# Unit solves moved to VectorE, x placed by products, weight sums on GpSimd, and spare products in TensorE's first waits

## The chip, the core and the metric

The kernel runs on one core of a Trainium2 chip. The metric is the time of one execution on the device in microseconds (us); the median of repeated runs is given. The core has five engines that run side by side and wait for each other through semaphores: TensorE (PE in the profile; its weight loads are PEld), VectorE (DVE), ScalarE (ACT), GpSimd (POOL) and SyncE (SP), which here only issues DMAs. Each engine works through its own queue in order.

## The reference

Two blocks follow each other. The first is a recurrence over 768 tokens for 4 batches x 8 heads with a state of 40 x 40:

```python
for t in range(S):
    y[:, :, t] = np.einsum('bhd,bhde->bhe', rt, state)
    Sa = np.einsum('bhde,bhe->bhd', state, at)
    state_decay = state * wt[:, :, None, :] - np.einsum('bhd,bhe->bhde', Sa, bt)
    state = state_decay + np.einsum('bhd,bhe->bhde', vt, kt)
```

Its output, 3072 tokens x 320 columns, is the x of the second block, a mixture of four experts with 1024 hidden columns, all in float32:

```python
p = domain_probs / (domain_probs.sum(-1, keepdims=True) + 1e-09)
for e in range(E):
    out += p[:, e:e + 1] * (np.maximum(x @ w1[e], 0.0) @ w2[e])
```

## The kernel before, in words

**Units.** The sequence is cut into 12 chunks of 64 tokens. A unit is one chunk of two batches, so there are 24 units (`NU`); unit u has chunk u // 2, and a chunk's two units hold its four batches. Units 0 and 1 start from an empty state (`q.start`).

**Stages of a unit.** `within` (L338) reads the inputs: it transposes W (pw), scans it along time on VectorE to products of decays (G, L346), transposes them back (pg), scales A, K and B with them (L359 to L392, with a reciprocal at L364), transposes the results (pAT, pNT, pKT) and makes the products inside the chunk: F and E (pfe), pev, and the causal scores pc. `substitute` (L437) solves a triangular system of 32 x 32 blocks: it copies the diagonal blocks out of F (L441), transposes them (M, L445), takes two rows at a time (L458, L461) and then steps through the rows, each step a product (L470) and a sum. On VectorE the sum is one reduction (L480), on GpSimd two additions (L483). Its argument `eng` says which of the two does it. `merge` (L490) joins the two blocks to the whole inverse: two VectorE transposes give Qc and QTc (L495, L497), GpSimd copies QTc to QT (L503), and TensorE products pY (L510) and pQ (L522) with ScalarE copies between give the rest of QT. `step` (L528) carries the state over the chunk: prn, psat (with pst, the part for the state), pxr, pdy, then on VectorE Y (L607 to L612) and the new state (L617, L618). At last it brings Y into `xT`, the layout in which the mixture reads x. In unit 0 this is done by twelve matrix instructions with a 0/1 matrix `pick` (pxT, L624) and a ScalarE copy (L628); in all others by twelve DMAs from SyncE (L636).

**The mixture.** Units 0 and 1 have a mixture of their own (`mixture_of_unit`): per expert `ups` makes the hidden layer in two pieces (ph, L651 and L659, then a Relu on ScalarE, L664), `down` multiplies it with w2 (po, L698), and VectorE adds the result to the output (L675, L677). From chunk 1 on both units of a chunk go together (`mixture_of_chunk`), and the down product is done in seven products of halves instead of eight (L763). For that, `add_weights` (L726) makes five sums and differences of the w2 halves of each expert once, 128 x 640 elements each, on VectorE (L735). They overwrite halves of w2 and buffers that held w1 pieces, `pick` and the probabilities, so each set comes after the last reader of those.

**Order.** The stages are generators. A list written out by hand at the end of the kernel runs them piece by piece: units 0 to 2 one by one, then a loop over u in which the work of units u to u+3 is interleaved. Between them `gap(n)` puts pieces of the mixture from the list `todo`: one piece where 4u+n is in `sparse`, else two; `weights_at` says in which gap which expert's weight sums are made. A scheduler may still move instructions, except those given to `keep_in_program_order`. TensorE's queue is strictly in the order that results. SyncE's queue holds the loads of a unit's six inputs, the w1 pieces, w2, the x placements and the stores in one line. Banks of PSUM for all small products come from one pool of five (`big`).

**Which engine solves.** Unit 0's solve is on VectorE, those of units 1 and 2 on GpSimd, those of units 3 to 5 on VectorE, the rest on GpSimd.

Of the kernel before, what the change touches and what calls it, by code (L numbers as in the profile page):

```python
# [15 lines left out]
def kernel(  # L16
# [320 lines left out]
    def within(q):  # L337
# [16 lines left out]
        nc.vector.tensor_tensor(out=q.gl[:], in0=q.gl[:], in1=G[:, :, L - 1:L], op=ALU.mult)  # L354
        yield

        pg = by(turn("pg", tok(G))[:], 64)[:, :, 0:D]
        gp = sb.tile([P, H, D], FP32, name="gp")
        ins = nc.vector.tensor_tensor(out=gp[:], in0=pg, in1=n["W"][:, :, 0:D], op=ALU.mult)  # L359
        if q.u == 1:  # L360
# [76 lines left out]
    def substitute(q, eng):  # L437

        blocks = sb.tile([P, H, Q], FP32, name="blocks")
        for i in range(P // Q):  # L440
            ins = eng.tensor_copy(out=blocks[quarter(i)], in_=q.F[quarter(i), :, quarter(i % 2)])  # L441
            tc.keep_in_program_order(ins)
        M = sb.tile([P, Q, Q], FP32, name="M")
        cols = blocks[:].rearrange("p h c -> p c h")[:, :, None, :].to_broadcast([P, Q, 4, H])
        ins = nc.vector.transpose(out=M[:], in_=cols)  # L445
        if q.u == 1 or eng is nc.vector:
            tc.keep_in_program_order(ins)


        pairs = M[:].rearrange("p (c two) r -> p c two r", two=2)  # L450
        on_diag = M[:].rearrange("p c r -> p (c r)")[:, Q + 1::2 * (Q + 1)]
        nc.vector.memset(on_diag, 0.0)

        Z = sb.tile([P, 4, Q // 4, Q], FP32, name="Z")
        q.Z = Z[:, 0]
        by_second = Z[:, 1:3].rearrange("p x k r -> p (x k) r")
        below = M[:].rearrange("p c r -> p (c r)")[:, 1::2 * (Q + 1)]
        nc.vector.tensor_tensor(  # L458
            out=by_second, in0=pairs[:, :, 1, :], in1=below[:, :, None].to_broadcast([P, Q // 2, Q]), op=ALU.mult,
        )  # L460
        nc.vector.tensor_tensor(out=pairs[:, :, 0, :], in0=pairs[:, :, 0, :], in1=by_second, op=ALU.add)  # L461
        at_once = eng is nc.vector
        for x in (0, 3) if at_once else (0,):
            tc.keep_in_program_order(eng.tensor_copy(out=Z[:, x], in_=unit_cols[:]))
        for j in range(0, Q, 2):
            if j == Q // 2:
                yield
            n, m = j // 4 + 1, Q - 1 - j
            here = 3 * (j // 2 % 2) if at_once else 0
            ins = eng.tensor_tensor(  # L470
                out=Z[:, 1:3, 0:n, j + 1:Q], in0=M[:, j:j + 2, None, j + 1:Q].to_broadcast([P, 2, n, m]),
                in1=Z[:, here, 0:n, j:j + 2].rearrange("p k x -> p x k")[:, :, :, None].to_broadcast([P, 2, n, m]),
                op=ALU.mult,
            )
            if j in (0, Q // 2):
                tc.keep_in_program_order(ins)
            z = Z[:, :, 0:n, j + 1:Q]
            if at_once:
                terms = z[:, 0:3] if here == 0 else z[:, 1:4]
                eng.tensor_reduce(out=z[:, 3 - here], in_=terms.rearrange("p x k r -> p k r x"), op=ALU.add, axis=AX.X)  # L480
            else:
                for x in range(1, 3):
                    eng.tensor_tensor(out=z[:, 0], in0=z[:, 0], in1=z[:, x], op=ALU.add)  # L483
        if at_once:

            odd, even = (Z[:, x].rearrange("p k (r four) -> p k r four", four=4)[:, :, :, 1:3] for x in (3, 0))
            eng.tensor_copy(out=even, in_=odd)
        yield
# [41 lines left out]
    def step(q, xT):  # L530

        st = [state[bb] for bb in q.b]
        if q.start:
            RH = q.EV
        else:
            p = banks("prn")
            prh = quadrants(p, 0, BY_TOKENS, D, lambda j, s, i: (
                s, i ^ s, j, of_pairs(q.AT, s, j, i), st[i][half(s), j, 0:D],
            ))

            psn = quadrants(p, NJ * D, BY_PAIRS, 64, lambda j, s, i: (
                s, d_half(j, s), 2 * i + j % 2, st[i][half(s), j, :], ident[half(s), half(s)],
            ))
            RH = RHs()
            for s in range(2):
                nc.vector.tensor_tensor(
                    out=of_slot(RH[:], s)[:, :, 0:D], in0=prh[s], in1=of_slot(q.EV[:], s)[:, :, 0:D], op=ALU.add,
                )
            SN = sb.tile([P, 2, 2 * 2, 64], FP32, name="SN", tag="step", bufs=3)
            for s in range(2):  # L550
                nc.scalar.copy(out=SN[:, s], in_=psn[s])
# [6 lines left out]
        ))  # L558
        SX = SXs()
        if not q.end:  # L560
            pst = quadrants(p, NJ * L, BY_TOKENS, D, lambda j, s, i: (
                i ^ s, i, j, q.QT[half(i ^ s), head(j, s), :], RH[half(i ^ s), head(j, s), 0:D],
            ))
        SaT = sb.tile([P, NJ, 2, L], FP32, name="SaT", tag="step", bufs=3)
# [53 lines left out]
                nc.vector.tensor_tensor(out=x, in0=x, in1=gl[:, :, i, :].to_broadcast([P, NJ, D]), op=ALU.mult)  # L618
        yield

        if q.u == 0:
            px = big("pxT")
            for n, (g, j) in enumerate(PLACES):
                nc.tensor.matmul(  # L624
                    out=px[:, g * P:(g + 1) * P], lhsT=pick[:, n, :], rhs=Y[:, j].rearrange("p i t -> p (i t)"),
                    start=(n == 0 or PLACES[n - 1][0] != g), stop=(n + 1 == len(PLACES) or PLACES[n + 1][0] != g),
                )
            nc.scalar.copy(out=xT, in_=px[:, 0:3 * P].rearrange("p (g t) -> p g t", g=3))  # L628
        for h in range(H if q.u else 0):
            lo = h * D  # L630
            while lo < (h + 1) * D:
                g, o = divmod(lo, P)
# [92 lines left out]
    def add_weights(e):  # L725

        b = {(q, x): of_w2(e, q, x) for q in range(2) for x in range(2)}
        for to, x, y, op in (
            (of_sums(e, 0), b[0, 0], b[1, 1], ALU.add),
            (of_sums(e, 1), b[0, 0], b[0, 1], ALU.add),  # L730
            (of_sums(e, 2), b[1, 0], b[1, 1], ALU.add),
            (b[0, 1], b[0, 1], b[1, 1], ALU.subtract),
            (b[1, 0], b[1, 0], b[0, 0], ALU.subtract),
        ):
            tc.keep_in_program_order(nc.vector.tensor_tensor(out=to, in0=x, in1=y, op=op))  # L735

    def mixture_of_chunk(qs, xT):

# [83 lines left out]
    def begin_step(u):  # L822
# [3 lines left out]
        q.xT = chunks_x[q.c][:, :, q.bp * P:(q.bp + 1) * P]  # L826
        return step(q, q.xT)

    ws = [within(units[u]) for u in range(3)]
    run(ws[0], 2)  # L830
    load(units[1], "ABKVR")
    run(ws[1], 1)
    run(ws[0], 2)
    run(substitute(units[0], nc.vector))
    run(ws[0], 1)
# [5 lines left out]
    for e in range(2):  # L841
        load_piece()
        load_piece()
        load_w2(e)
    run(ws[1], 1)
    load(units[2], "ABK")
    load_piece()
    for e in range(2, E):
# [3 lines left out]
    run(ws[1], 1)  # L852
    run(s)
    run(ws[1], 1)
    run(substitute(units[1], nc.gpsimd))
    mixture_of_unit(units[0])
    normalize()
    run(ws[2], 1)
    run(ws[1])
    mix(1)  # L860
    run(ws[2], 2)
    mix(1)
    run(ws[2], 2)
    mix(1)
    m, s = merge(units[1]), begin_step(1)
    run(m, 1)
    run(ws[2], 1)
    load(begin(3), srcs)
    run(substitute(units[2], nc.gpsimd))
    run(m)  # L870
    mix(1)
    run(s, 2)
    mix(1)
    w_next, solve = ws[2], iter(())

    sparse = [4 * u + n for u in range(1, 4) for n in range(4)] + [16]

    weights_at = {4 * 2 + 2: 0, 4 * 3 + 0: 1, 4 * 3 + 2: 2, 4 * 3 + 3: 3}
    for u in range(1, NU):
        q = units[u]  # L880
        m = s_next = w = iter(())
# [74 lines left out]
```

## Time and profile before

| what | value |
|---|---|
| median of 3 runs | 1180.26 us (1180.16 to 1181.2) |
| span of the profiled run | 1179.7 us |
| TensorE busy | 1129.8 us, 96% |
| weight loads | 1005.5 us, 85% |
| VectorE busy | 698.1 us, 59% |
| ScalarE busy | 364.5 us, 31% |
| GpSimd busy | 462.4 us, 39% |
| DMA | 108.03 MB, mean 92 GB/s |

The page also cuts the span into 40 slices of 29.5 us. A digit is a busy share in tenths; PEclk is the clock granted to TensorE.

```profile
PE   4789996999999999999999999999999999999998
DVE  6633787856646655755656566566466557543333
POOL 4165000044734734625536436447347356250000
PEclk8689997999999999999999999999999999999999
DMA  4782633333333333342342332333333331221330
```

The first eight slices differ from the rest: TensorE has gaps there, its clock is below full in several slices, and the DMAs are fullest in the third. A matrix product of float32 with a 128 x 128 weight shows up as two instructions in the profile, so twelve in the profile are six in the kernel.

### The profile page before, as it was taken

What the parts mean: (1) busy time and instruction counts of PE and PEld (TensorE: products, weight loads), DVE (VectorE), ACT (ScalarE), POOL (GpSimd) and SP (SyncE); (2) the same over time, 40 slices, a digit from 0 to 9 for tenths busy, and PEclk for the clock granted to TensorE, in tenths of its full rate; (3) what the DMA queues carried; (4) which work ended last, traced back from release to release, by engine and by line L of the source; (5) the groups of instructions that cost most, each with busy time, mean ns of one, the idle gap of its engine ahead of it and who ended that gap; (6) DMA issues with size and microseconds to landing.
All of it is one profiled execution on the core that took longest, in us unless ns stands there. A gap on an engine that the chain in (4) does not pass through costs nothing.

```text
span 1179.7 us, 38554 instructions
## 1 busy us (share of the span) xinstructions
PE 1129.8 (96%) x16272; PEld 1005.5 (85%) x16272; DVE 698.1 (59%) x1503; ACT 364.5 (31%) x910; POOL 462.4 (39%) x1200
## 2 busy tenths in 40 slices
PE   4789996999999999999999999999999999999998
PEld 3668785899989989898998989999888998988887
DVE  6633787856646655755656566566466557543333
ACT  2323342333332333333333333333323333221110
POOL 4165000044734734625536436447347356250000
PEclk8689997999999999999999999999999999999999
DMA  4782633333333333342342332333333331221330
GB/s 67 200 239 68 141 64 86 78 108 68 95 94 84 96 95 81 92 103 73 95 95 63 108 89 73 107 78 89 90 93 90 93 91 58 76 86 51 103 89 12
DMA packets 220246, 108.03 MB, mean 92 GB/s; under 512 B 164090, under 2 KB 193450, under 8 KB 220074
## 3 DMA queue, kind: packets, MB, share of 16 engines
q1 hardware_dynamic: 220074, 105.56, 34.9%
q8 instruction: 129, 2.11, 0.7%
q14 instruction: 43, 0.35, 0.1%
HBM read 97.04 MB, written 3.93 MB: 86 GB/s over the span
## 4 chain that ended last, share of the span: by engine, by line
PE 86%; DVE 5%; POOL 3%; SPq 2%; issue 2%; DMA 1%; ACT 1%; POOLq 0%; DVEq 0%; ACTq 0%
PE p L763 27%; PE ph L659 27%; PE ph L651 8%; PE pdy L326 3%; PE po L698 2%; PE pfe L326 2%; PE prn L326 2%; POOL Z L483 2%; PE psat L326 2%; PE pxr L326 2%; SPq L188 1%; PE pQ L522 1%; PE pY L510 1%; POOL Z L470 1%; PE pc L326 1%
## 5 line engine op out<-in xcount | busy, mean ns | idle before, releaser
L659 PE MATMUL ph<-xT,w1p 128*128 128x256 f32 (+1 forms) x1520 | 342.8, 378 | 0.2 <-issue 0.2
L659 PEld LDWEIGHTS ph<-xT,w1p 128*128 128x128 f32 x1520 | 274.1, 190 | 62.8 <-issue 25.5
L757 DVE TENSOR_TENSOR a<-hs 128x512 f32<-128x512 f32 x220 | 149.9, 698 | 196.4 <-ACT hs L664 196.3
L483 POOL TENSOR_TENSOR Z<-Z 128x54 f32<-128x54 f32 (+14 forms) x640 | 217.4, 340 | 50.2
L664 ACT ACTIVATE hs<-ph 128x512 f32<-128x512 f32 (+1 forms) x208 | 117.4, 564 | 324.6 <-PE ph L659 323.5
L470 POOL TENSOR_TENSOR Z<-M,Z 128x62 f32<-128x62 f32 (+7 forms) x320 | 154.2, 482 | 89.5 <-DVE M L461 66.0
L677 DVE SCALAR_TENSOR_TENSOR osb<-p,gate,osb 128x320 f32<-128x320 f32 (+1 forms) x242 | 108.4, 486 | 110.4 <-PE p L763 103.2
L763 PE MATMUL p<-sums,a 128*128 128x160 f32 x1056 | 164.8, 299 | 0.0
L763 PEld LDWEIGHTS p<-sums,a 128*128 128x128 f32 x1056 | 152.9, 190 | 2.2
L441 POOL COPY blocks<-F 32x256 f32<-32x256 f32 x80 | 32.3, 404 | 276.6 <-ACT F L416 274.1
L651 PE MATMUL ph<-xT,w1p 64*128 64x256 f32 (+1 forms) x760 | 109.2, 399 | 4.9 <-issue 4.9
L503 POOL COPY QT<-QTc 32x256 f32<-32x256 f32 x96 | 37.7, 393 | 170.6 <-DVE QTc L497 160.7
L763 PE MATMUL p<-w,hs 128*128 128x160 f32 x704 | 102.8, 299 | 0.0
L763 PE MATMUL p<-w,a 128*128 128x160 f32 x704 | 102.8, 299 | 0.0
L763 PEld LDWEIGHTS p<-w,hs 128*128 128x128 f32 x704 | 100.3, 190 | 2.2
L763 PEld LDWEIGHTS p<-w,a 128*128 128x128 f32 x704 | 98.0, 190 | 0.0
L651 PEld LDWEIGHTS ph<-xT,w1p 64*128 64x128 f32 x760 | 67.3, 188 | 17.7 <-issue 7.8
L445 DVE STREAM_TRANSPOSE M<-blocks 128x1024 f32<-128x1024 f32 x24 | 47.1, 1964 | 26.0 <-POOL blocks L441 25.9
L364 DVE RECIPROCAL gp<-gp 128x320 f32<-128x320 f32 x24 | 51.5, 2145 | 0.0
L416 ACT COPY F<-pfe 128x256 f32<-128x256 f32 x48 | 15.5, 375 | 107.8 <-PE pfe L326 107.8
L592 ACT COPY RS<-pxr 64x256 f32<-64x256 f32 x88 | 32.2, 366 | 44.3 <-issue 25.3
L698 PE MATMUL po<-w,hs 128*128 128x320 f32 x128 | 44.0, 500 | 0.0
(140 smaller groups left out, 1406.8 us busy)
## 6 DMA issues: line engine op xcount, KB each, us to landing
w1p<-in_moe_w_dram SPq DMA_DIRECT2D x95, 512.0 KB
w1p<-in_moe_w_dram SPq DMA_DIRECT2D x190, 64.0 KB
w<-in_moe_w_dram SPq DMA_DIRECT2D x4, 1280.0 KB
sums<-in_moe_w_dram SPq DMA_DIRECT2D x9, 512.0 KB
natW<-in_w_dram SPq DMA_DIRECT2D x48, 80.0 KB
natA<-in_a_dram SPq DMA_DIRECT2D x48, 80.0 KB
natB<-in_b_dram SPq DMA_DIRECT2D x48, 80.0 KB
natK<-in_k_dram SPq DMA_DIRECT2D x48, 80.0 KB
```

The costliest lines, as they stand in the source:

```text
L326: nc.tensor.matmul(out=p[row][half(col), lo + at * out_cols:lo + (at + 1) * out_cols], lhsT=lhsT, rhs=rhs, start=(n == 0), stop=(n == len( ...
L364: nc.vector.reciprocal(out=gp[:], in_=gp[:])
L445: ins = nc.vector.transpose(out=M[:], in_=cols)
L470: ins = eng.tensor_tensor(out=Z[:, 1:3, 0:n, j + 1:Q], in0=M[:, j:j + 2, None, j + 1:Q].to_broadcast([P, 2, n, m]), in1=Z[:, here, 0:n, j: ...
L483: eng.tensor_tensor(out=z[:, 0], in0=z[:, 0], in1=z[:, x], op=ALU.add)
L651: nc.tensor.matmul(out=ph[i][:, f, :], lhsT=w1.last[i * DT:(i + 1) * DT, f, :], rhs=xT[i * DT:(i + 1) * DT, 2, :], start=(f == 0), stop=False,
L659: nc.tensor.matmul(out=ph[i][:, f, :], lhsT=w1.main[:, g, at * P:(at + 1) * P], rhs=xT[:, g, :], start=False, stop=(g == 1 and f == HF // ...
L664: nc.scalar.activation(out=h[:, i * HF // 2:(i + 1) * HF // 2, 0:n], in_=ph[i][:], func=ACTF.Relu,)
L677: nc.vector.scalar_tensor_tensor(out=to, in0=p, scalar=sc, in1=to, op0=ALU.mult, op1=ALU.add)
L698: nc.tensor.matmul(out=po[:], lhsT=hs[e][f // HF][:, f % HF, 0:P], rhs=w2_sb[e][:, f, :], start=(f == 0), stop=(f == NF - 1),)
L757: nc.vector.tensor_tensor(out=t[:], in0=x, in1=y, op=op)
L763: nc.tensor.matmul(out=p[:, n * HD:(n + 1) * HD], lhsT=a[:, f, :], rhs=b[:, f, :], start=(f == 0), stop=(f == HF - 1),)
```

## The change

The change has six parts, all in the work of the first units.

1. The solves of units 1 and 2 run on VectorE too, so all of the first six do. Of the four block copies of such a solve, VectorE makes two and ScalarE two.
2. x of units 0 to 3 (`q.c < 2`) is placed by products; DMAs place it from unit 4 on. `pick`, which shares a buffer with the weight sums of expert 3, lives longer for this.
3. The weight sums are made on GpSimd, and in other gaps: 9, 11, 12 and 14 in place of 10, 12, 14 and 15.
4. `keep_warm` puts spare products of the identity with itself on TensorE, whose result is not used: 14 before unit 0's pw, 12 before its pg, 2 before pAT, and 72 behind unit 1's pg, ahead of unit 0's pY. They are there for the time in which TensorE waits for unit 0's first stages and its solve.
5. In units 0 and 1 pst has banks of its own instead of sharing psat's.
6. The hand-written order is changed: unit 0's mixture comes ahead of unit 1's solve and starts with three pieces, unit 1's merge comes earlier, unit 2's solve is begun and carried over into the loop as the later ones are, and the gaps of one piece run from 4 to 17. The first transpose of unit 2's pg keeps its place.

```diff
-        pg = by(turn("pg", tok(G))[:], 64)[:, :, 0:D]
+        pg = by(turn("pg", tok(G), q.u == 2)[:], 64)[:, :, 0:D]
...
-            ins = eng.tensor_copy(out=blocks[quarter(i)], in_=q.F[quarter(i), :, quarter(i % 2)])
-            tc.keep_in_program_order(ins)
+            move = nc.scalar.copy if eng is nc.vector and i >= 2 else eng.tensor_copy
+            tc.keep_in_program_order(move(out=blocks[quarter(i)], in_=q.F[quarter(i), :, quarter(i % 2)]))
...
+        placed = q.c < 2
...
-            pst = quadrants(p, NJ * L, BY_TOKENS, D, lambda j, s, i: (
+            at = (banks("pst"), 0) if q.start else (p, NJ * L)
+            pst = quadrants(*at, BY_TOKENS, D, lambda j, s, i: (
...
-        if q.u == 0:
+        if placed:
...
-        for h in range(H if q.u else 0):
+        for h in range(0 if placed else H):
...
-            tc.keep_in_program_order(nc.vector.tensor_tensor(out=to, in0=x, in1=y, op=op))
+            tc.keep_in_program_order(nc.gpsimd.tensor_tensor(out=to, in0=x, in1=y, op=op))
...
+    warm = big("warm")
+    def keep_warm(n):
+        for _ in range(n):
+            ins = nc.tensor.matmul(out=warm[:, 0:P], lhsT=ident[:], rhs=ident[:], start=True, stop=True)
+            tc.keep_in_program_order(ins)
...
-    run(ws[0], 2)
+    keep_warm(14)
+    run(ws[0], 1)
+    keep_warm(12)
+    run(ws[0], 1)
     load(units[1], "ABKVR")
     run(ws[1], 1)
+    keep_warm(2)
...
     run(ws[1], 1)
+    keep_warm(72)
     load(units[2], "ABK")
...
-    run(substitute(units[1], nc.gpsimd))
     mixture_of_unit(units[0])
+    run(substitute(units[1], nc.vector))
     normalize()
...
-    run(substitute(units[2], nc.gpsimd))
+    solve = substitute(units[2], nc.vector)
+    run(solve, 1)
...
-    sparse = [4 * u + n for u in range(1, 4) for n in range(4)] + [16]
-    weights_at = {4 * 2 + 2: 0, 4 * 3 + 0: 1, 4 * 3 + 2: 2, 4 * 3 + 3: 3}
+    sparse = range(4 * 1, 4 * 4 + 2)
+    weights_at = {4 * 2 + 1: 0, 4 * 2 + 3: 1, 4 * 3 + 0: 2, 4 * 3 + 2: 3}
```

## The prediction

> **What bounds the kernel now.** I read the table of windows first, because the change touches only the first six of 24 units. Columns: window, its length, then busy time and count of matmul, weight load, VectorE, ScalarE, GpSimd, then granted clock, DMA share, GB/s.
>
> ```profile
> 0.00:42.00 42.00, 18.03 (x327) 15.05 (x328) 29.43 (x77) 10.36 (x27) 14.42 (x48) 0.74 0.40 67
> 42.00:80.00 38.00, 33.48 (x506) 28.65 (x498) 17.19 (x39) 13.66 (x34) 20.05 (x57) 0.90 0.95 280
> 80.00:125.00 45.00, 43.80 (x694) 34.18 (x693) 16.34 (x36) 13.84 (x41) 19.69 (x57) 0.87 0.44 109
> 125.00:200.00 75.00, 66.31 (x1200) 54.92 (x1199) 62.97 (x161) 27.74 (x77) 3.15 (x8) 0.93 0.38 75
> 200.00:240.00 40.00, 35.02 (x463) 29.42 (x464) 30.57 (x79) 12.38 (x32) 1.58 (x4) 0.87 0.37 98
> 240.00:1140.00 900.00, 898.26 (x12876) 811.50 (x12875) 525.35 (x1079) 282.97 (x698) 403.52 (x1026) 1.00 0.33 87
> ```
>
> From 240 to 1140 us TensorE is busy 898.3 of 900 us at full clock: no wait is left to take away there, and added products cost their full time. Before 240 it idles 43.4 us (240 less 196.6 busy) and runs at a lowered clock part of the time. So every microsecond won before 240 moves the end by one. The waits of TensorE name the idle time (waiter, releaser, total, times, longest):
>
> ```profile
> PE pY L510 <- DVE QTc L497: 16.2, 3, 11.9
> PE pNT L294 <- DVE n_tok L389: 7.2, 4, 4.7
> PE ph L651 <- issue: 4.9, 2, 4.5
> PE pw L294 <- DMA natW<-in_w_dram: 4.8, 1, 4.8
> PE pRT L294 <- DMA natR<-in_r_dram: 2.1, 3, 0.8
> PE pdy L326 <- ACT RS L592: 1.6, 2, 1.4
> ```
>
> pY waits for solves: 11.9 us in unit 0, 3.9 in unit 1. The timeline shows the other places (start, length, engine, line):
>
> ```profile
> 186.45 1.13 PE L326 MATMUL pc<-RT,VT 64*64 64x64 f32 x32
> 111.54 0.69 PE L326 MATMUL pc<-RT,VT 64*64 64x64 f32 x32
> 109.34 8.03 SPq L636 DMA_DIRECT2D xT<-Y  x11
> 197.12 3.28 DMA xT<-Y
> 203.37 3.02 PE L651 MATMUL ph<-xT,w1p 64*128 64x256 f32 x8 [4.52 <-issue]
> ```
>
> The same 32 products take 0.69 us at full clock and 1.13 after a wait. The x of a unit goes as 12 DMAs through SyncE, and each set holds up the loads queued behind it; in unit 3 the mixture itself waits 4.5 us for x. Pricing the lowered stretches by their full-clock twins gives about 11 us lost before 48 us (four transposes take 0.60 at 47 us, 1.09 before) and 15 us at 79-89, 115-122, 184-197, 203-207 and 221-224.
>
> **What the Trainium skill says.** "TensorE: Matmul & The Clock Gate", What's actually happening: the array runs at half clock after an idle window of about 3.4 us and at full clock after such a window of sustained work. The trace agrees in kind: the waits of 3.9, 4.7 and 4.5 us are each followed by slow products. "GPSIMD Engine Reference", Elementwise — side-by-side cycle accounting: two inputs cost about 2.6 cycles an element at 1.2 GHz, 2.2 ns. The solve's rows on GpSimd give 1.8 (0.29 us for 62 elements, 0.45 for 152). "SBUF — State Buffer", Who interferes with whom: a VectorE instruction with two SBUF inputs and a GpSimd one that reads SBUF exclude each other. Here GpSimd alone pays: its L470 stretches to 1.38 us from 0.39, while the 24 VectorE L458 stay within 691 to 694 ns.
>
> **The change part by part.**
>
> Spare products. A product shows as two profile instructions: pxT's six are twelve and took 1.50 us, 0.111 us apiece; at the low clock four transposes give 0.24. The 14 ahead of pw are 28 such: from 1.7 us, when the identity is ready, at 0.24 until one cold window or two have passed (5.1 to 8.5 us), then at 0.111. They end between 6.8 and 8.4; I take 7.1, where W lands at 4.76. The 12 ahead of pg take 24 x 0.111 = 2.7 us and the scan path between 1.9, so pg ends at 10.7 for 8.95: **1.75 us late**. The 72 are 144 instructions, 16.0 us at full clock, and start behind pc and pg near 23.2 (before 22.8; ScalarE's two extra copies stand ahead of VT). They end near 39.2, so **pY waits for them**, not for the solve: QTc comes at 34.8 (34.56 + 1.75 - 0.9 for faster pNT to pfe - 0.6 for block copies: VectorE's four took 1.17, now two, with two of 0.38 beside on ScalarE). One cold window at their start would add 1.7 us; cold throughout, 19. What they buy is a full clock after them: pY 0.45, pQ 0.75, psat/pst 1.3, pxr 0.7, pdy 1.4, transposes 1.1, 5.7 us. pY 4.6 late less 5.7 is 1.1 earlier; part of it is lost to ScalarE and VectorE steps between, so unit 1's F comes at 51.0 for 51.3. Sum of unit 0: **nothing**, between +4 (fill cold at first, clock lost again) and -3. The separate bank for pst lets SaT be copied before pst ends, within the 5.7; pinning pg's first transpose moves nothing I can price.
>
> Unit 1's solve. On GpSimd 57.6 to 77.0; on VectorE unit 0 took 22.8 to 33.4. From F: 5.9 us to Z (ET, blocks, M, scan, three big operations), 10.7 of Z, 0.9 of VC, gates and a down add 1.8, transposes 1.1, and about 1 of gaps: QTc at 72.3 instead of 78.1. TensorE meets pY at 75.1, after two ups (5.3 each), two downs (4.5) and 4.5 of small products from 51.0, so the 3.9 us wait and its cold down (4.5 us at 79-89) go. Weights do not hold it: 42 to 80 us has the DMAs 95% busy at 280 GB/s, and counting bytes in SyncE's order from 40 us the second piece of ups(2) lands near 75.6. TensorE ends ups(2) at 81.6, before at 95.4, with 4.65 us of other work put off: **9.1 us ahead**.
>
> Next limits: SyncE starts unit 3's loads at 81.6 as before, now with six piece DMAs ahead (3.5 us), so R lands near 100.4, and TensorE wants it at 98.8: 1.6 back. Unit 2's F at 87.5 puts Y of unit 1 at 107.7 on VectorE, behind the solve, and pxT could start at 104.9: 2.8 back. The placement itself adds 1.4, a wait of 1.2 at pQ and the cold down at 116 go (2.7), PSUM banks 1.4 back: **5.6 us ahead** at 117.
>
> Placed x in units 1 to 3: 36 DMAs at 0.716 us, 26 us of SyncE, gone, with 9.2 us in which SyncE held for unit 1's state. Added: 1.4 us of TensorE each, 0.48 us of ScalarE beside it. New wait: pxT needs Y, and behind it on TensorE stand the rest of a down, pAT, pNT, pKT and the next pY. Y stands on VectorE after nearly the whole solve and the 2.15 us reciprocal. In unit 2 VectorE ran without a gap from ET at 123.7 to Y's last product at 146.2, 22.5 us; now 1.2 less in copies and reordered state adds. TensorE gets from pfe's end to pxT in 18.9 us (psat 1.1, down 4.5, pw/pev/pxr 2.2, ups 5.3, three transposes 1.6, pdy 1.75, half a down 2.3); Y is there 1.0 + 21.3 after pfe: about 3.4 us of wait per unit. Units 2 and 3: 2 x (3.4 + 1.4) = 9.6 us lost, and 3.4 for the clock after those waits (1.7 each).
>
> Weight sums. Off VectorE: 20 x 0.74 = 15 us, of which 3.8 held unit 3's n_tok (wait 4.7). On GpSimd each 640 elements cost 0.2 + 640 x 1.8 ns = 1.35 us, 2.3 if blocked: 7 to 12 us for five. Queued behind sums 0 to 2 stand unit 4's QT copies, for which psat waits; the sums follow downs about 20 us ahead of pY of unit 4, so they are hidden. Taken at 0.
>
> Waits of before that go from 123 to 240: natR, pNT 2.9, n_tok 4.7, cold after it 4.7: 12.3. x of unit 3 4.5, cold 2.65, RS and cold pdy 3.2: 10.3. Unit 0's mixture now starts with three pieces at once and two later gaps give one piece for two; that reorders products and adds none.
>
> Sum: 5.6 - 9.6 - 3.4 + 12.3 + 10.3 = 15.2 us. 1180.3 - 15.2 = **1165 us**.
>
> **The rivals.**
> - *All waits go.* VectorE, 15 us lighter, delivers Y in time and R lands with the pieces: 6.8 + 3.4 + 2.8 + 1.6 more, 1150. For: VectorE idles 7.5 us at 115-122. Against: its gapless 25 us chain in unit 2. Below that little is left: start, DMA-bound stretch and tail stay.
> - *Clock and VectorE spoil half.* The spare products start cold and the chain after them cools again, 4 lost; units 1 to 4 each wait 1.5 us more for Y or QTc: 1175. For: a 1.4 us gap at 220 was already followed by slow pdy.
> - *The sums shut VectorE out.* Each GpSimd sum stops VectorE for its whole 1.35 us in the solve chains: 20 x 1.35 = 27, giving 1192, **slower**; a fill cold throughout (19 late) gives 1184. Against: 691 to 694 ns of L458 beside a running GpSimd solve, and a clock that rose under dense products in every stretch.
>
> **How the numbers follow.** Forecast 0.50, all waits gone 0.20, half spoilt 0.23, slower cases 0.07. Range 1150 to 1178: the first three with their spread, and most of the fourth left out. Faster 0.92, same 0.02, slower 0.06.
>
> **What would show it.** Right: unit 0's pY waiting for spare products until about 39, QTc of unit 1 near 72, pxT waiting 2 to 4 us for Y, no wait for x at the first chunk, 240 to 1000 unchanged. Wrong: spare products done before QTc (then more is won), slow products (1.1 us for 32) between 39 and 50 us, L458 or L470 on VectorE lengthened beside the sums, or new idle time past 240.

## The result, and the profile after

The changed kernel takes 1194.51 us (1193.35 to 1194.87), the kernel before beside it 1180.21 us (1179.94 to 1181.2): a ratio of 1.0118, 95% interval 1.01 to 1.0135. It is 14.3 us **slower**; the prediction was 15.2 us faster.

Four rows of the page after, in 40 slices:

```profile
PE   7898996899999999999999999999999999999998
DVE  6477567746666566566466466557557557543433
POOL 4000073116536436436347347346356355250000
PEclk8999998979999999999999999999999999999999
```

A slice is 29.8 us. GpSimd (POOL) is idle in slices 2 to 5, as its two solves have left it, and has a 7 in slice 6, 149 to 179 us: the weight sums. VectorE (DVE) has 7 and 7 in slices 3 and 4, where it had 3 and 3: the solves it took over. TensorE (PE) drops to 6 in slice 7, just after GpSimd's 7; slices 7 and 9 also have a lower clock.

The table of windows of the kernel after (window, length, busy time and count of matmul, weight load, VectorE, ScalarE, GpSimd, then clock, DMA share, GB/s):

```profile
0.00:42.00 42.00, 35.11 (x389) 33.68 (x391) 28.82 (x75) 8.27 (x19) 13.74 (x48) 0.92 0.41 67
42.00:80.00 38.00, 33.34 (x501) 27.94 (x495) 21.65 (x67) 13.29 (x36) 1.41 (x4) 0.96 0.92 275
80.00:125.00 45.00, 40.78 (x713) 34.27 (x712) 28.83 (x77) 16.39 (x43) 1.75 (x5) 0.96 0.58 133
125.00:200.00 75.00, 60.55 (x1042) 51.49 (x1040) 53.02 (x128) 26.47 (x76) 25.21 (x19) 0.93 0.30 69
200.00:240.00 40.00, 34.26 (x598) 29.11 (x599) 28.38 (x81) 15.53 (x40) 9.13 (x9) 0.98 0.34 81
240.00:1140.00 900.00, 897.85 (x12977) 809.44 (x12976) 524.11 (x1082) 284.29 (x702) 405.20 (x1030) 0.99 0.34 86
```

From 240 us on TensorE is as full as before (897.85 of 900 for 898.26). So the loss is made before that: pfe of unit 6 starts at 259.0 for 245.6, 13.4 us behind, and pfe of unit 7 is behind by the same 13.4. From 42 to 80 us the clock rose from 0.90 to 0.96 as intended, yet TensorE idles 4.7 us there as before (4.5). From 125 to 240 us it idles 14.45 + 5.74 = 20.2 us, where the kernel before idled 8.69 + 4.98 = 13.7. TensorE's waits name what the idle time is:

```profile
PE ph L654 <- ACT hs L667: 7.1, 2, 4.4
PE pNT L294 <- DVE n_tok L389: 6.3, 2, 4.3
PE ph L654 <- DVE osb L680: 4.5, 1, 4.5
PE pxT L627 <- DVE Y L610: 4.2, 1, 4.2
PE pxT L627 <- DVE Y L615: 3.1, 2, 2.1
PE pKT L294 <- issue: 2.8, 1, 2.8
PE pY L510 <- DVE QTc L497: 0.4, 1, 0.4
```

pY's 16.2 us for the solves, the 4.5 for x, the 4.8 for natW and the 2.1 for natR are gone, as meant (natW's only because spare products stand in its place: pw starts at 7.2 us for 4.8). In their place stand waits that the kernel before did not have at all: the mixture's own ph waits 11.6 us for hs and osb, pxT 7.3 us for Y.

Two places of the trace carry the rest. First, TensorE's timeline about the spare products (start, length, line, operation, then in brackets the idle time before it):

```profile
24.06 17.61 PE L837 MATMUL warm<-ident 128*128 128x128 f32 x144
41.60 0.69 PE L510 MATMUL pY<-QTc,F 32*32 32x32 f32 x32
...
53.22 0.33 PE L294 MATMUL pKT<-ident,k_tok 128*128 128x128 f32 x1 [2.79 <-issue]
53.38 2.06 PE L627 MATMUL pxT<-Y,sums 128*128 128x128 f32 x12
```

The spare products run 7 us past the end of the solve (QTc is there at 34.6), so pY comes at 41.6 for 34.7. It takes 0.69 us instead of 1.07: warm (at full clock), but 6.9 us late. At 50.4 TensorE stalls for 2.79 us; the profile names nothing that it waits for. After that the clock is low again (pxT 2.06 us, about 1.5 at full clock).

Second, GpSimd's and then VectorE's timeline between 157 and 183 us:

```profile
157.48 1.75 POOL L503 COPY QT<-QTc 32x256 f32<-32x256 f32 x4 [37.37 <-DVE QTc L497]
159.32 4.54 POOL L738 TENSOR_TENSOR sums<-w 128x640 f32<-128x640 f32 x3
163.81 3.04 POOL L738 TENSOR_TENSOR w<-w 128x640 f32<-128x640 f32 x2
...
174.44 5.44 POOL L738 TENSOR_TENSOR sums<-w 128x640 f32<-128x640 f32 x3
179.84 3.11 POOL L738 TENSOR_TENSOR w<-w 128x640 f32<-128x640 f32 x2
```

```profile
170.19 2.87 DVE L442 COPY blocks<-F 32x256 f32<-32x256 f32 x2
...
175.35 1.19 DVE L458 TENSOR_TENSOR Z<-M 128x512 f32<-128x512 f32 x1
176.57 1.92 DVE L461 TENSOR_TENSOR M<-M,Z 128x512 f32<-128x512 f32 x1
178.41 3.16 DVE L464 COPY Z<-unit_cols 128x256 f32<-128x256 f32 x2
181.49 1.54 DVE L470 TENSOR_TENSOR Z<-M,Z 128x62 f32<-128x62 f32 x1
```

Three sets of five sums stand in one row behind the QT copies of unit 3, which wait for QTc until 157.5. They meet the start of unit 4's solve, and there VectorE's instructions take 2.87, 1.19, 1.92, 3.16 and 1.54 us; the same ones elsewhere take 0.57, 0.69, 0.69, 0.49 and 0.21. That is 8.0 us in one solve.

### The profile page after: what moved, and what is told of

It is laid out like the page before. It is cut to its first block, busy times and chain, and to the rows that moved or that the text cites. A ratio compares the mean times of both kernels' runs of the same rounds, so it can differ in the third digit from the quotient of the medians.

```text
span 1193.1 us, 38940 instructions
## 1 busy us (share of the span) xinstructions
PE 1150.5 (96%) x16508; PEld 1030.2 (86%) x16508; DVE 705.8 (59%) x1549; ACT 370.2 (31%) x925; POOL 456.4 (38%) x1114
## 3 DMA queue, kind: packets, MB, share of 16 engines
q1 hardware_dynamic: 218520, 104.97, 34.7%
## 4 chain that ended last, share of the span: by engine, by line
PE 87%; DVE 8%; POOL 2%; issue 1%; ACT 1%; ACTq 0%; DVEq 0%; POOLq 0%
PE ph L662 27%; PE p L766 27%; PE ph L654 8%; PE pdy L326 3%; PE pfe L326 2%; PE warm L837 2%; PE prn L326 2%; DVE Z L480 2%; PE psat L326 2%; PE pxr L326 2%; PE po L701 1%; DVE Z L470 1%; PE pQ L522 1%; PE pY L510 1%; PE pc L326 1%
## 5 line engine op out<-in xcount | busy, mean ns | idle before, releaser
L483 POOL TENSOR_TENSOR Z<-Z 128x54 f32<-128x54 f32 (+14 forms) x576 | 199.4, 346 | 45.1
L470 POOL TENSOR_TENSOR Z<-M,Z 128x108 f32<-128x108 f32 (+14 forms) x288 | 140.5, 488 | 80.5 <-DVE M L461 59.4
L442 POOL COPY blocks<-F 32x256 f32<-32x256 f32 x72 | 28.3, 393 | 266.8 <-ACT F L416 264.5
L445 DVE STREAM_TRANSPOSE M<-blocks 128x1024 f32<-128x1024 f32 x24 | 47.2, 1968 | 26.8 <-POOL blocks L442 22.7
L368 ACT COPY RT<-pRT 128x512 f32<-128x512 f32 x24 | 14.1, 586 | 86.1 <-PE pRT L294 86.0
```

The lines of the kernel that those rows point to most:

```text
L470: ins = eng.tensor_tensor(out=Z[:, 1:3, 0:n, j + 1:Q], in0=M[:, j:j + 2, None, j + 1:Q].to_broadcast([P, 2, n, m]), in1=Z[:, here, 0:n, j: ...
```

## The experiments

All ratios are to the kernel before, measured beside each version on the same chip; it took 1180.2 to 1181.2 us in all of them. Repeated runs of one kernel spread by some 5 us to either side there, so the interval of the ratio is what decides. Each version has one trace, of one of its runs, so times at single places of two traces can differ by what belongs to the run and not to the edit. "pfe(1)" is pfe of unit 1, and so on.

| kernel | median us | ratio, 95% interval |
|---|---|---|
| after | 1194.51 | 1.0118, 1.01 to 1.0135 |
| after, sums on VectorE | 1188.26 | 1.0059, 1.0033 to 1.0085 |
| after, no 72 | 1184.68 | 1.0043, 1.003 to 1.0056 |
| both of these ("**base**" below) | 1181.86 | 1.0011, 0.9997 to 1.0024 |
| before, sums on GpSimd | 1179.03 | 0.9987, 0.997 to 1.0003 |
| before, x of units 1 to 3 placed | 1183.36 | 1.0023, 1.0012 to 1.0035 |
| before, 40 spare products | 1180.14 | 0.9989, 0.9973 to 1.0006 |
| base, solves of units 1, 2 on GpSimd | 1189.56 | 1.0069, 1.0046 to 1.0091 |
| base, all block copies on VectorE | 1183.38 | 1.0013, 0.9993 to 1.0033 |
| base, x of units 1 to 3 by DMA | 1190.99 | 1.0088, 1.0058 to 1.0118 |
| base, gaps like before | 1183.30 | 1.0029, 1.0018 to 1.0041 |
| base, gaps, copies, x by DMA | 1182.40 | 1.0017, 1.0002 to 1.0032 |
| the same, no spare products at all | 1182.31 | 1.0011, 0.9996 to 1.0025 |
| after, no 72, sums in the gaps of before | 1180.59 | 0.9994, 0.9982 to 1.0006 |
| base, 40 spare products | 1184.40 | 1.0020, 1.0001 to 1.0038 |
| base, one piece from gap 14 to 15 | 1178.73 | 0.9988, 0.9977 to 0.9999 |
| the same, 40 spare, copies on VectorE | 1181.75 | 1.0012, 0.9998 to 1.0026 |
| after, no 72, gaps of before, piece moved | **1178.17** | **0.9979, 0.9968 to 0.999** |
| the same, copies on VectorE | 1183.19 | 1.0021, 1.0011 to 1.003 |

### The sums and the 72, undone one by one and together

```diff
-            tc.keep_in_program_order(nc.gpsimd.tensor_tensor(out=to, in0=x, in1=y, op=op))
+            tc.keep_in_program_order(nc.vector.tensor_tensor(out=to, in0=x, in1=y, op=op))
```

> The changed kernel with the weight sums back on VectorE (same gaps). Theory 'lock': the fifteen GpSimd sums at 159-183 us hold up VectorE's solve of unit 4 (its block copies, L458, L461, L464 and first L470 took 8.0 us more than their usual lengths), and TensorE waits behind it twice (4.5 and 4.4 us); on VectorE the sums cost 3.8 us a set, partly in its idle time: 1183 to 1188, L458 back at 0.69 us everywhere. Rival 'start': the loss is the spare products before 60 us; then this run stays within 2 us of the changed kernel, 1193 to 1196.

1188.26: 6.2 us back, and ph's wait for osb is gone. The wait of 4.3 for n_tok stays, so it is not the sums' doing. Not all of the 6.2 is the sums' either. They begin at 159 us in the kernel after, but this run's trace is ahead long before: pfe(1) starts at 52.8 for 55.4 and pfe(3) at 127.1 for 130.2, since the stall of 2.79 us and the slow products behind it are not in it. Of the 7.6 us by which pfe(6) is earlier (251.4 for 259.0), 3.1 were there before the first sum.

```diff
-    keep_warm(72)
```

> The changed kernel without the 72 spare products ahead of unit 0's pY. Theory 'start': they end at 41.6 us while QTc was there near 35, so pY comes near 35.5; the chain behind it runs at the low clock and is some 5 us longer, so unit 1's F comes 1 to 4 us earlier than in the changed kernel: 1190 to 1193.5. Rival 'clock': the slow chain eats all of it or more: 1194 to 1197. If the lock is the whole loss, nothing but that small shift shows here.

1184.68: 9.8 us back, more than the 6.9 by which pY was late. TensorE now waits for the solve again, and pY is cold:

```profile
34.94 1.07 PE L510 MATMUL pY<-QTc,F 32*32 32x32 f32 x32 [10.62 <-DVE QTc L497]
```

pfe(1) ends at 48.9 for 57.4: 8.5 us of the 9.8. The stall of 2.79 us ahead of the last pKT product is not in this run's trace either, so part of the 8.5 is the stall's and not that of the late pY. A like one, 2.8 us without a named releaser, stands in pfe of unit 2 in two later runs (at 82.9 with the gaps like before, at 87.3 with 40 spare products in the base). What it is, and whether it belongs to a kernel or to a single run, stays open.

> The changed kernel with the sums on VectorE and without the 72 spare products. If the two causes are separate the gains add: 1180 to 1186. If they share the same slack (an earlier start only waits longer for loads), it equals the sums-on-VectorE run within 1 us.

1181.86, and what is left of the change **equals the kernel before**. The hoped-for gain is not hidden by these two; it is missing as well. Together they give 12.7 us back, alone 6.2 and 9.8, which is over 3 us more. That the losses themselves overlap is not shown: the stall stands in the trace of the kernel after alone, and each single undoing may have counted it. Counted from the other side, the sums on GpSimd cost 2.8 us (1184.68 less 1181.86) and the 72 cost 6.4 (1188.26 less 1181.86).

### Single parts put into the kernel before

Only the sums on GpSimd, in before's own gaps:

> The kernel before with only the weight sums moved to GpSimd, in its own gaps. Lock: each set of five takes about 7.7 us on GpSimd and stops VectorE's two-input and copy instructions in the solves of units 3 to 5; VectorE is spared 3.8 us a set, so the net is 0 to 10 us slower: 1181 to 1190, with L458, L464 or L470 on VectorE stretched beside a sum. Rival (VectorE is spared and GpSimd alone pays): 1174 to 1180, and no VectorE instruction longer than before.

1179.03, no difference. The time is the rival's, the lengthened instructions are the lock's: VectorE is lengthened there too (single L461, L464 and L470 up to 1.92, 1.63 and 1.55 us), but spared the 3.8 us a set that the sums take on VectorE.

Only the placement, units 1 to 3:

```diff
-        if q.u == 0:
+        if q.c < 2:
...
-        for h in range(H if q.u else 0):
+        for h in range(0 if q.c < 2 else H):
```

> The kernel before with only x of units 1 to 3 placed by products. Waits that should go: x for the first chunk 4.5 us and the slow products behind it 2.7, natR 2.1; added: 3 x 1.4 us of products and up to 1 to 3 us a unit of waiting for Y. 1172 to 1178 if the placement is a gain by itself; 1180 or more if the wait for Y eats it (rival: every part of the change that leans on VectorE loses).

1183.36, slower by 2.7 us. The largest new wait of this run:

```profile
PE pxT L624 <- DVE Y L612: 9.8, 2, 5.1
```

x and natR are waited for no more, but pxT, in the middle of TensorE's queue, waits 4.6 and 5.1 us for Y and is cold itself after each wait (2.90 and 2.93 us, about 1.5 at full clock). A DMA's transit ran beside TensorE's queue; the product stops it.

Only a fill that ends inside the solve:

```diff
+    keep_warm(40)
```

> The kernel before with only 40 spare products behind unit 1's pg, 80 instructions: [...]done by 34 us, just ahead of QTc at 34.6. Theory 'too many': the fill is right in kind and the 72 only end too late: pY not later than 35.2, then 0.69 us products, unit 1's F 3 to 5 us earlier; but the next limit (the weights' DMAs, 95% busy to 80 us) takes part of it: 1175 to 1179. Rival: the clock falls again in the chain's gaps, 1180.

1180.14, no difference. pY comes at 35.5, 0.8 us later than before but warm (0.69 us), and pfe(1) starts 1.1 us earlier; the end does not move.

### What the rest of the change is worth

Units 1 and 2 solved on GpSimd again, in the base:

```diff
-    run(substitute(units[1], nc.vector))
+    run(substitute(units[1], nc.gpsimd))
...
-    solve = substitute(units[2], nc.vector)
+    solve = substitute(units[2], nc.gpsimd)
```

> The changed kernel without the 72 spare products, sums on VectorE, and the solves of units 1 and 2 back on GpSimd (order as changed). If VectorE's solves of units 1 and 2 are a gain, this is slower than with them by 3 to 10 us (their GpSimd solve is 19.4 us for 10.7 and pY now comes earlier in TensorE's queue): 1184 to 1192. Rival (VectorE is what these units wait for): 1176 to 1182.

1189.56: the faster solves are worth 7.7 us in this order. pY of unit 1 waits 2.9 us for its solve again, that of unit 2 3.5.

The block copies of a solve all on VectorE:

```diff
-            move = nc.scalar.copy if eng is nc.vector and i >= 2 else eng.tensor_copy
+            move = eng.tensor_copy
```

> The changed kernel without the 72 spare products, sums on VectorE, and all four block copies on VectorE. In units 3 to 5 ScalarE's two copies stand behind SaT and SX and M starts 1.2 to 1.9 us late, for 0.6 us saved on VectorE: this version gains 0.6 to 1.3 us a unit in units 3 to 5 where VectorE's chain is the limit, loses 0.6 in unit 0: 1178 to 1181.5. Rival: no difference within 1 us, since TensorE waits there for other things.

1183.38: no difference that the interval can tell, and no gain. M no longer waits 1.2 to 1.9 us for ScalarE's copies, VectorE has two copies more, and ph waits 7.6 us for hs where the base waits 5.3.

x of units 1 to 3 by DMA, in the base:

```diff
-        placed = q.c < 2
+        placed = q.u == 0
```

> The kernel after with sums on VectorE and without the 72 spare products, where only unit 0's x is placed by products; units 1 to 3 go by DMA as before. Its base took 1181.9. Theory (placing x costs in any order: 3 x 1.4 us of products and the waits for Y, 2.7 us in the order of before): 1178 to 1180, with the waits for natR and for x coming back in small pieces. Rival (in the changed order Y is there in time, since the base waits only 0.8 us for it, while the DMAs hold up the loads in SyncE's queue): 1183 to 1187, with waits of TensorE for natR or x of 3 us and more.

1190.99: the rival was right in kind, and more so than it said. In the order of before the placement cost 2.7 us; in this order taking it away costs 9.1. Its new wait:

```profile
PE ph L654 <- DMA xT<-Y: 7.3, 3, 5.4
```

The base waits 0.8 us for Y at pxT; with DMAs the mixture waits 7.3 for x instead, of which 5.4 stand at 193 to 198 us, behind SyncE's twelve DMAs of 188.4 to 197.3. **The same edit has two signs**, by whether Y is there when TensorE's queue comes to it.

### The last wait: n_tok of unit 5's period

Between pfe(5) and pNT the changed order leaves two ups beside VectorE's chain, where before had three. First the gaps of before, with 2 pieces at the start for 3:

```diff
-    mix(3)
+    mix(2)
...
-    sparse = range(4 * 1, 4 * 4 + 2)
-    weights_at = {4 * 2 + 1: 0, 4 * 2 + 3: 1, 4 * 3 + 0: 2, 4 * 3 + 2: 3}
+    sparse = range(4 * 1, 4 * 4 + 1)
+    weights_at = {4 * 2 + 1: 0, 4 * 2 + 3: 1, 4 * 3 + 1: 2, 4 * 3 + 3: 3}
```

In this and the next two runs the first two sets of sums come one piece of the mixture earlier than they may, so that part of unit 1's hidden layer is made from overwritten w1 pieces; the amount of work is the same, but ph can wait for the sums, 1.5 us at most.

> The same base, with one ups fewer ahead of unit 1's step (2 for 3 at the start of unit 0's mixture) and gap 17 giving two pieces again, so that three ups stand between pfe(5) and pNT of that period as in the kernel before; two sets of weight sums go one gap later for it. Theory (the 4.3 us wait for n_tok at 221 us is a lack of 4.7 us of TensorE work beside the 25 us chain on VectorE, and the slow clock after it costs 2 to 3 more): 1175 to 1178, with that wait under 1 us. Rival (the piece taken from the start opens the same wait earlier, at pY of unit 1, which waits 1.4 us in the base): 1180 to 1184.

1183.30, and the wait is 4.9 us instead of under 1: a miss. VectorE's timeline after pfe(5) shows why that wait is no shorter:

```profile
217.04 2.29 DVE L738 TENSOR_TENSOR sums<-w 128x640 f32<-128x640 f32 x3
219.25 1.55 DVE L738 TENSOR_TENSOR w<-w 128x640 f32<-128x640 f32 x2
```

The fourth set of sums now stands in gap 15, in the middle of the solve. What TensorE got as cover, VectorE got as work: 3.8 us in the chain that TensorE waits for. Earlier in this trace pxT waits 10.4 us for Y, for 0.8 in the base, and a stall without a named releaser takes 2.8: the piece taken from the start is missed as well. (The wait of 1.4 us at pY, which the text above gives to unit 1, stands in the base's trace at pY of unit 4, at 194.4.)

> The same base with three edits together: x of units 1 to 3 by DMA, the gaps of the second run, all four block copies on VectorE. If the losses are separate: 1181.9 less 2.5 for x, 5 for the gaps, 0 to 1 for the copies: 1173 to 1176, below the kernel before. Rival (what one edit wins, the next wait takes): 1178 to 1182.

1182.40: no gain from three edits together. It does not show 9 us for x by DMA as in the base, so what that costs hangs on the gaps as well.

> The third run without the other 28 spare products (14, 12 and 2). If they only delay pg (pY of unit 0 came at 35.4 in the base and at 34.7 before): 0.5 to 1 us less than the third run. Rival (they hold the clock up through the first stages): 1 to 2 us more.

1182.31: the 14, 12 and 2 spare products of the first 24 us cost nothing and bring nothing. pY of unit 0 comes at 34.8; with them, in the traces without a fill ahead of it, it comes at 34.6 to 35.8. Without them TensorE waits there for W (5.0 us) and G (2.5).

Then one piece moved without touching the sums:

```diff
-            mix(1 if at in sparse else 2)
+            mix({14: 0, 15: 2}.get(at, 1 if at in sparse else 2))
```

> Sums on VectorE, none of the 72, and gap 14 gives no piece, gap 15 two. In TensorE's queue this moves half an ups, 2.0 us, from ahead of pfe of unit 5 to behind it. Theory (TensorE's wait of 4.3 us for n_tok of that period is the lack of products beside the gapless VectorE chain): the wait falls by 2 us, 1178.5 to 1180.5 for 1181.9. Rival (the piece taken away opens a wait at pQ or pfe, or the wait is made good later): 1181.5 to 1183.

1178.73 for the base's 1181.86: the wait falls by 1.0 us only, to 3.3. pfe(5) is 2.7 us earlier, 2.0 of which is the work moved behind it; pfe(6) is 2.1 earlier, and the end 3.1 by the medians (the two intervals overlap by a hair).

### Engine or place, and how many spare products

```diff
-    weights_at = {4 * 2 + 1: 0, 4 * 2 + 3: 1, 4 * 3 + 0: 2, 4 * 3 + 2: 3}
+    weights_at = {4 * 2 + 2: 0, 4 * 3 + 0: 1, 4 * 3 + 2: 2, 4 * 3 + 3: 3}
```

> The kernel after without the 72 spare products, sums on GpSimd, but in the gaps of before (10, 12, 14, 15) in place of 9, 11, 12, 14. With sums in the gaps of after it took 1184.7; with sums on VectorE 1181.9; in the order of before the move to GpSimd cost nothing. Theory (the loss comes from the place: three sets in one row behind QT copies beside the solve of unit 4, in later gaps they are spread out): 1180 to 1182, and no VectorE copy over 2 us beside them. Rival (each sum holds VectorE wherever a solve runs): 1184 to 1187, with several L442, L461, L464 of 1.5 to 3 us.

1180.59 for 1184.68 with the sums on GpSimd in both: **the loss needs the place as well as the engine**. On GpSimd in these gaps the sums cost no more than on VectorE (1181.86). The third set now stands behind the QT copies of unit 4, at 190 us; only two sets lie between 151.4 and 166.6, so that of unit 4's solve, which begins after pfe(4) at 161.2, only the first steps meet them (two L442 in 2.88 us). The other two sets meet the start of unit 5's solve (two L442 in 2.30 us, L458 1.12). That is 4.5 us in two solves, for 8.0 in one. One line each of the durations (min/median/max in ns) of the copy L464 on VectorE, after and then in this run:

```profile
L464 DVE COPY Z<-unit_cols x12: 284/286/1621, 22.4 to 221.3; 128x256 f32<-128x256 f32 x12
```

```profile
L464 DVE COPY Z<-unit_cols x12: 285/286/289, 23.1 to 207.1; 128x256 f32<-128x256 f32 x12
```

```diff
-    keep_warm(72)
+    keep_warm(40)
```

> The kernel after with sums on VectorE and 40 spare products in place of 72 ahead of pY of unit 0. With 72 it took 1188.3, with none 1181.9. Theory (only what runs past the solve costs; 40 end near 33, so pY keeps its time of 35 us and the products behind it run at full clock): 1180 to 1182, pY at 34.9 to 35.6, and unit 1's pfe ends 1 us earlier than with none (49.5). Rival (spare products delay the chain in any number): 1183 to 1186.

1184.40 for 1181.86 with none; the intervals overlap. pY is on time (35.1) and pfe(1) 2.2 us earlier than in the base, pfe(3) 0.2 us. So a fill that ends in time does no harm at pY. What it wins is gone within two units of this trace; but one of the stalls of 2.8 us stands between, in pfe(2), so whether the gain would last without it is not shown.

### Put together

> The third run with 40 spare products ahead of pY of unit 0 and all block copies on VectorE: what the runs so far suggest as the best of both orders. If the gains add (2 from the piece, 1 from the clock after the 40, 1.2 from the block copies, on 1181.9): 1177 to 1179, below the kernel before. Rival (each of them is made good by the next wait, as in all runs around 1180): 1180 to 1182.

1181.75: with the 40 and the copies on VectorE the moved piece's gain is not seen; that their gains add is refuted, and which of the two takes it is not separated.

> The kernel after without the 72 spare products, weight sums on GpSimd in the gaps of before, and with gap 14 giving no piece and gap 15 two. Alone, the sums' gaps gave 1180.6 and the moved piece 1178.7 on a base of 1181.9. If the two add: 1177 to 1178.5, ratio to before 0.997 to 0.999. Rival (the moved piece wins nothing where VectorE has the sums off its queue): 1180 to 1181.

1178.17, ratio 0.9979 (0.9968 to 0.999): 3.0 us below the kernel before by the medians, 2.5 by the ratio. This is **the version furthest below both kernels**: the change without the 72, with the sums in the gaps of before and one piece moved. The only other interval wholly below 1, by a hair, is that of the moved piece alone. It is one of the nineteen versions of the table, so the lowest of many, though its time had been forecast. In its trace the sums still hold VectorE up, by 6.4 us in the solves of units 4 and 5 (one L461 takes 1.91 us).

> The same with all four block copies of a solve on VectorE, which takes ScalarE out of the start of the solves (M waited 1.2 to 1.9 us for ScalarE's copies): if that shortens the chain that pNT waits for, 1 us less than the run before it. Rival (ScalarE's copies took as much off VectorE as they made it wait, as in the run with VectorE's sums): the same within 1 us.

1183.19, 5.0 us more, where the same edit cost the base nothing. VectorE's timeline of this run at unit 5's solve, and GpSimd's beside it:

```profile
200.99 6.33 DVE L442 COPY blocks<-F 32x256 f32<-32x256 f32 x4
207.35 1.99 DVE L445 STREAM_TRANSPOSE M<-blocks 128x1024 f32<-128x1024 f32 x1
209.53 1.25 DVE L458 TENSOR_TENSOR Z<-M 128x512 f32<-128x512 f32 x1
```

```profile
199.45 3.07 POOL L738 TENSOR_TENSOR w<-w 128x640 f32<-128x640 f32 x2
202.45 4.72 POOL L738 TENSOR_TENSOR sums<-w 128x640 f32<-128x640 f32 x3
```

Four copies that take 1.17 us in the kernel before take 6.33 beside these sums: each waits for one. The transpose after them, still beside sums (the next two run from 207.1 to 210.2), keeps its 1.99 us. With two copies on ScalarE only two can be caught. Here, too, the delay reaches TensorE through ScalarE: ph waits 10.3 us for hs, 5.9 in the run before.

## Why the prediction was wrong, point by point

Between 1165 and 1194.5 lie 29.5 us. About 15 of them are the stretch from 123 to 240 us, where the sum counted removed waits at their full length; that is the step that failed most. Another 12.7 are two terms that the sum put at nothing, the spare products and the weight sums. Under 2 us are left over.

**Spare products: taken at nothing, 6.4 to 9.8 us.** Predicted: start 23.2, end 39.2, pY waits for them and not for the solve, sum "nothing, between +4 and -3". Measured: 24.06 to 41.67, and pY waits for them: the mechanism was right, two sizes were not. The first is the length of the row, 17.6 us for 16.0; with the start 0.9 later, pY came 2.4 us later than forecast. Three stretches of the kernel after (columns as above, the clock third from the end):

```profile
24.00:27.00 3.00, 3.00 (x17) 3.00 (x16) 2.73 (x9) 0.00 (x0) 0.00 (x0) 0.51 0.21 30
27.00:50.50 23.50, 22.02 (x367) 20.83 (x365) 13.69 (x40) 4.39 (x13) 1.57 (x4) 1.00 0.55 139
53.20:57.40 4.20, 4.18 (x78) 3.84 (x79) 0.00 (x0) 1.06 (x2) 0.00 (x0) 0.62 1.08 325
```

The row starts at half clock; the step had named that, at 1.7 us, and left it out of its sum. The second is the 5.7 us of regained clock that were to pay for it. The clock did come back and stayed at 1.00 beyond the row, through pY to pKT and over gaps of 0.46 and 0.55 us, until the stall of 2.79 us. "TensorE: Matmul & The Clock Gate" of the Trainium skill, What's actually happening, gives an idle window of about 3.4 us as what halves the clock; the short gaps agree with that, while here a stall of 2.79 us was followed by slow products too. But the regained clock is worth less than 5.7. From the start of pY to the end of pfe(1) TensorE took 15.9 us before, 14.2 in the base and 13.0 to 14.2 in the other traces with the new order and nothing ahead of pY, and 12.2 in the run with the 72 and the sums on VectorE, whose trace has no stall there. So the 72 win 2 us at most and bring pY 6.4 us later (41.7 for 35.4); at the end they cost 6.4 (1188.26 less 1181.86), and 9.8 beside the sums on GpSimd, where the stall may be counted in. Unit 1's F came at 58.1, where the step had 51.0. The 28 early ones were forecast to make pg 1.75 late; they cost nothing measurable.

**Unit 1's solve on VectorE: right in kind, the size in part by luck.** Predicted pY of unit 1 at 75.1 and 5.6 us ahead at 117. The step's own terms (9.1 - 1.6 - 2.8 - 1.4 + 2.7 - 1.4) add to 4.6, which would have made the forecast 1166. The base has pY at 75.3, and its pfe(3) stands at 121.7 for 122.0 with one ups of 5.3 us more done: 5.6 ahead. The run with the solves back on GpSimd puts 7.7 us on it. Two terms were off in opposite directions: the wait for R of unit 3, forecast at 1.6, measured 3.3 in the base, and the one for Y of unit 1, forecast at 2.8, is not there. In the kernel after, the late start took the gain: pY at 83.1.

**The weight sums: taken at nothing on a reading that compared nothing.** Rival 3, that sums shut VectorE out, was set aside because the 24 L458 stayed within 691 to 694 ns "beside a running GpSimd solve". In the trace of before, none of the 24 runs beside a GpSimd instruction. In a solve on GpSimd the order forbids it: GpSimd's rows wait for L461, which follows L458. VectorE's and then GpSimd's timeline of before for unit 6:

```profile
251.38 0.69 DVE L458 TENSOR_TENSOR Z<-M 128x512 f32<-128x512 f32 x1
252.11 0.69 DVE L461 TENSOR_TENSOR M<-M,Z 128x512 f32<-128x512 f32 x1
```

```profile
252.95 0.29 POOL L470 TENSOR_TENSOR Z<-M,Z 128x62 f32<-128x62 f32 x1 [3.30 <-DVE M L461]
```

So "here GpSimd alone pays" had no evidence. VectorE instructions that did meet GpSimd's solve were lengthened in the same trace, by little. For the update of the state the view gives (min/median/max in ns):

```profile
L618 DVE TENSOR_TENSOR state<-state,gl x44: 318/384/456, 46.9 to 1002.8; 128x160 f32<-128x160 f32 x44
```

The ten of the 44 that meet no GpSimd instruction take 318 to 322 ns, the others 381 to 456. A row of GpSimd's solve is short, though (L470 0.39 us at the median); a sum holds on for 1.55 us. "SBUF — State Buffer", Who interferes with whom, says that whoever issues first gets the pair of ports for the whole instruction, the other blocks, and that copies can contend too; the trace after agrees (2.87 us for two copies, 1.92 for one L461), and the four copies in 6.33 us show it cleanest. The size was not rival 3's 27 us: 8.0 us in one solve, and at the end 2.8 without the 72, 6.2 with them, where the stall may be counted in. The duration was small too: "GPSIMD Engine Reference", Elementwise — side-by-side cycle accounting, gives 2.6 cycles an element, which at its 1.2 GHz makes an estimate of 1.39 us for 640; I took 1.35 from the rows of the solve; measured 1.55. The other half of the step, "queued behind sums 0 to 2 stand unit 4's QT copies", looked at what stands behind the sums and not at what stands ahead: unit 3's QT copies held three sets back until the next solve began.

**Placed x.** Predicted 3.4 us of wait for Y in units 2 and 3 and 2.8 in unit 1, with 1.4 of products each. Measured after: 4.2 at unit 1, 2.1 and 1.0 later. In the kernel before alone it was 4.6 and 5.1: undersized there, oversized in the base (0.8). What the step missed is that the wait is no property of the edit.

**The removed waits: the step that failed most.** The sum took 12.3 + 10.3 = 22.6 us for the waits of before that go between 123 and 240 us, less 13.0 for placement. At 117 the base was the forecast 5.6 us ahead; at pfe(6) it is level with before (245.4 for 245.6). So this stretch gave -5.4 and not +9.6. Two lines of the table of windows for the base:

```profile
125.00:200.00 75.00, 66.84 (x1164) 56.23 (x1166) 61.76 (x156) 27.33 (x75) 5.03 (x8) 0.95 0.38 81
200.00:240.00 40.00, 34.45 (x496) 28.15 (x488) 27.80 (x78) 14.07 (x37) 1.58 (x4) 0.83 0.30 75
```

TensorE idles 8.16 + 5.55 = 13.7 us here, as in the kernel before (13.7), with 2.8 us of placing added. By TensorE's timeline of the two, waits of 13.7 us went: natR 2.1, n_tok 0.75 and 4.72, x 4.52, RS 1.6. Others came, 13.6 us: ph for hs 2.65 and 2.66, Y 0.8, VC 0.6, QTc 1.35, G 0.7, RS 0.55, n_tok 4.29, and after this last one the clock was low. Removed waits were counted as if nothing stood next to them.

Two of the new waits can be followed to the reorder that the step said "adds none". VectorE's chain of some 25 us from pfe to n_tok set the period in unit 5, and TensorE's cover beside it had fallen by one ups: the reorder added no product and moved one out of the place where it covered a wait. The waits for hs come by another way. ScalarE in the base:

```profile
134.78 0.74 ACT L595 COPY RS<-pxr 64x256 f32<-64x256 f32 x2 [4.43 <-DVE SX L333]
135.55 0.38 ACT L667 ACTIVATE hs<-ph 128x256 f32<-128x256 f32 x1
```

VectorE makes SX between the rows of its solve, RS waits 4.43 us for it, and the Relu that writes hs stands behind RS in ScalarE's queue. In the kernel before the Relus of this period (126.0 to 129.8) stand ahead of RS (136.4). No run moved them back, so this is read from the traces and not tested. That the lost cover is a cause is shown in part, by the moved piece: 1.0 us of the wait and 3.1 us at the end by the medians. No run gave back the 15 us between the forecast and the measurement in this stretch.

**The signs named in advance.** "L458 or L470 on VectorE lengthened beside the sums" came. "Slow products (1.1 us for 32) between 39 and 50 us" did not: the clock was full from 27 to 50.5 us, and the slow products (pfe 1.13 us) came behind the stall, at 55.4.

## What to carry to other kernels

A wait that is removed was worth here its length less the next wait in the same stretch: before counting one, lay the other engines' chains beside what TensorE has to do in that period, piece by piece. A spare product has to end before the work it warms for is ready; ending 7 us late here cost 6 to 10. Evidence that two engines do not disturb each other counts only from instructions that ran at the same time. Work moved to GpSimd is to be judged by what stands ahead of it in that queue and by what VectorE runs when it gets its turn, for a long GpSimd instruction can hold up one VectorE instruction after another, once per sum.

## What the runs showed of the hardware

- A GpSimd sum of two inputs in SBUF, 128 x 640 and 1.55 us long, held up VectorE instructions that began beside it by up to 1.4 us each: copies of one input (0.28 to 1.67 us an L442, 0.29 to 1.63 an L464) as well as products of two (0.69 to 1.92 an L461, 0.21 to 1.55 an L470). The transpose L445 (1.91 to 2.01 us in all runs) was not lengthened beside them, nor was the addition RH, one of whose two inputs lies in PSUM (0.31 to 0.33 us).
- A long row of 128-column float32 spare products took 0.122 us an instruction over 17.6 us and 0.134 over 10.7, because both rows began at half clock. At full clock the longer one ran 91 instructions in 9.9 us, 0.109 us apiece.
- The granted clock stayed at 1.00 over gaps of 0.46 and 0.55 us after such a row; after a stall of 2.79 us the next 4.2 us had 0.62.
